# A wider tile cleared by GpSimd between two indirect transfers, in an attention-and-experts kernel

## The chip, the cores and the metric

One core of one Trainium2 chip runs the program. The metric is the device time of one launch in microseconds; lower is better. Two runs of the kernel before took 1105.46 and 1108.3 us, so its median is 1106.88 us. The profiled execution is a third run with its own time, 1112.21 us.

## The reference

Four batches of 10048 rows of 128 columns go through agent attention, and its rows then go through a two-level mixture of experts. Cut to what matters:

```python
a2k = sm(agents, k)                 # 49 agents attend to the keys
agent_v = a2k @ v
q2a = sm(q, agents)                 # each query attends to the 49 agents
x = (q2a @ agent_v).reshape(-1, 128)

g_idx = argmax(x @ w_group, axis=1)             # 4 groups, the best one per row
e_idx = argmax(xg @ w_expert[g], axis=1)        # 4 experts in it, the best one per row
h  = np.maximum(xg[mask_e] @ w1[g, e], 0.0)     # 128 -> 1024
ye = h @ w2[g, e]                               # 1024 -> 128
out[tok_idx] = combined[:, None] * ye           # by the row's two softmax weights
```

## The kernel before

**The natural part.** The rows of a batch lie in 79 tiles of 128. Each batch has one main expert, to which most of its rows go. For it the rows are taken in their natural order, four tiles (512 rows) at a time; this is what `natural` and `run` do. Such a unit has eight rounds. In a round `first` makes one 128 x 512 block of the hidden layer on TensorE (PE), two matmuls with a weight load each; ScalarE (ACT) writes its high half `hh` and VectorE (DVE) its low half `hl`, both in 16 bits. `second` multiplies the block of an earlier round with the second weights, twelve matmuls with a weight load each, into the accumulator `po`. So a round is 14 matmuls and 14 loads on PE. The finished unit is scaled by DVE into `oo` and leaves by an ordinary DMA from SyncE's queue.

**The rows that belong to other experts.** For the last batch handled (`LB`) the last part of the program, from about 770 us on, works by expert: 17 tiles (`TAKEN`) of up to 512 rows each. `fetch` (L1055) gathers a tile by four indirect DMAs from GpSimd (POOL), one for 128 rows of 200 bytes each, from a table `erow` in DRAM into `er` (five buffers). `turn` (L1082) transposes them on PE, `run` does the eight rounds, and `scatter` (L1092) scales the result into `oo` (three buffers, shared with the natural units) and sends it out by four indirect DMAs from POOL, 128 rows of 512 bytes each.

**The clearing between them.** After each of these indirect DMAs `apart` (L1074) puts one `memset` of a small tile `gap` on POOL. Nothing reads `gap`. `keep_in_program_order` keeps the DMA and the memset in the order in which they are written:

```python
def apart(ins):
    tc.keep_in_program_order(ins)
    tc.keep_in_program_order(pool.memset(gap, 0.0))
```

There are 68 gathers, 68 scatters and 136 memsets. POOL runs its instructions in order.

**The order of the work.** `build` ends with the loop that sets this order (L1236 to L1248): three tiles are fetched ahead, then two natural units of the batch before run, then for each of the 17 tiles its rounds run and the tile three places later is fetched; four more natural units are put between the 17. The rounds run with a lag (`LAG` is 8), so that a tile's `scatter` is issued while the next tile's rounds run. On POOL this gives 16 gathers with a memset behind each, four gathers with none between them (their memsets stand later in POOL's order), and from then on groups of four scatters and four gathers, each followed by its memset; at the end there are groups of four scatters alone.

Of the kernel before, what the change touches and what calls it, by code (L numbers as in the profile page):

```python
# [10 lines left out]
F32 = mybir.dt.float32  # L11
F16 = mybir.dt.float16
# [8 lines left out]
P = 128  # L21
# [111 lines left out]
def build(ctx, tc, qT, kT, v, agT, wr, w1, w2, cpk, out):  # L133
# [7 lines left out]
    const = ctx.enter_context(tc.tile_pool(name="const", bufs=1))  # L141
# [895 lines left out]

    done = [0]
    ring = []
    gap = const.tile([P, 16], F32, name="gap")  # L1040

    def place(b, col):
        for lo, hi, gidx, sidx in state[b]["idx"]:
# [235 lines left out]
```

## Time and profile before

| | |
|---|---|
| median of two runs | 1106.88 us |
| the profiled execution: device time | 1112.21 us |
| the profiled execution: span of its instructions | 1110.4 us |
| mean granted TensorE clock over the span | 0.936 |
| PE busy | 965.7 us (87%) |
| weight loads on PE's second row (PEld) | 753.1 us (68%) |
| DVE busy | 768.5 us (69%) |
| ACT busy | 639.3 us (58%) |
| POOL busy | 438.2 us (39%) |
| of which 136 memsets of `gap` | 17.9 us |
| first and last indirect DMA from POOL | 770.3 and 1102.7 us |

The device time is 1.8 us more than the span. Times in the views count from the span's start. In a row of the timeline the columns are the start, the duration, the engine, the line and operation, and in brackets how long the engine sat idle before it and what ended that; "issue" means that the profile shows nothing that it waited for. In a row of the windows each engine has its busy time in the stretch and in round brackets the number of its instructions; PE's matmuls and its weight loads (PEld) are counted apart, and after them come the granted clock, the share of DMA time, and GB/s.

### The profile page before, as it was taken

Reading aid. Unit: us, or ns where it says so; the run is one execution under the profiler, and the core shown is the slowest. Engines: PE = TensorE matmul, PEld = TensorE weight load, DVE = VectorE, ACT = ScalarE, POOL = GpSimd, SP = SyncE. Lnnn points to the kernel's source line nnn. Section 1 sums busy time; section 2 is a strip of 40 time slices with the busy share of each in tenths; the row PEclk is TensorE's granted clock in tenths of the full one; section 3 lists DMA queues with packets and bytes.
Section 4 is the critical chain, followed back from the end, with each engine's and each line's share of the span. In section 5 each row is a group of like instructions: output and inputs, shape, how many; then the busy total and the mean of one; then the engine's idle time right before and its main releaser. Section 6 shows DMA issues by size and latency. Waiting matters only on the chain.

```text
span 1110.4 us, 31414 instructions
## 1 busy us (share of the span) xinstructions
PE 965.7 (87%) x13174; PEld 753.1 (68%) x13174; DVE 768.5 (69%) x1475; ACT 639.3 (58%) x1144; POOL 438.2 (39%) x772
## 2 busy tenths in 40 slices
PE   4868989899999999989998999999597887877894
PEld 3747767678777887867787887776275665555673
DVE  6578889876989777797975679998263444434452
ACT  5355677798567787667766875544252333433441
POOL 3242283683054384026225520002506535454514
PEclk9969999999999999999998999999698788888988
DMA  9552254440475351157333112232243212232210
GB/s 297 164 184 84 73 150 142 137 146 21 141 237 151 103 153 37 33 183 264 110 99 99 53 31 79 94 125 81 63 181 104 99 62 100 65 102 65 91 55 31
DMA packets 104423, 124.58 MB, mean 112 GB/s; under 512 B 6743, under 2 KB 88152, under 8 KB 101328
## 3 DMA queue, kind: packets, MB, share of 16 engines
q1 hardware_dynamic: 99920, 116.57, 33.1%
q0 software_dynamic: 4352, 5.91, 2.0%
q8 instruction: 105, 1.72, 0.6%
q14 instruction: 46, 0.38, 0.1%
HBM read 89.01 MB, written 33.75 MB: 111 GB/s over the span
## 4 chain that ended last, share of the span: by engine, by line
PE 21%; issue 18%; POOL 13%; DVE 11%; ACT 1%; DMA 1%; POOLq 0%; SPq 0%; ACTq 0%
PE po L128 9%; PE ph L128 6%; POOL out L1097 6%; PE at L128 5%; DVE hl L128 5%; POOL er L1060 5%; POOL gap L1076 1%; POOL xl L237 1%; DVE oo L128 1%; DVE oh L128 1%; DMA w2f<-w 1%; DVE oa L128 0%; ACT hh L128 0%; DVE za L128 0%; DVE wbuf L128 0%
## 5 line engine op out<-in xcount | busy, mean ns | idle before, releaser
L128 DVE SCALAR_TENSOR_TENSOR hl<-ph,hh 128x512 f16<-128x512 f32 (+1 forms) x656 | 435.4, 678 | 246.0 <-ACT hh L128 182.6
L128 PEld LDWEIGHTS <-hh 128*128 128x128 f16 x5200 | 439.7, 100 | 197.7 <-issue 59.3
L128 ACT ACTIVATE hh<-ph 128x512 f16<-128x512 f32 (+1 forms) x656 | 381.1, 592 | 286.2 <-PE ph L128 249.3
L128 PE MATMUL po<-wbuf,hh 128*128 128x128 f16 x4816 | 495.5, 223 | 24.8 <-issue 24.3
L128 PE MATMUL po<-wbuf,hl 128*128 128x128 f16 x2408 | 451.9, 223 | 12.3 <-issue 12.2
L128 PE MATMUL ph<-et,wbuf 98*128 98x512 f16 (+1 forms) x1040 | 317.7, 385 | 25.7 <-DVE hl L128 20.3
L237 POOL TENSOR_TENSOR xl<-xf,xh 128x256 f16<-128x256 f32 (+1 forms) x288 | 191.2, 699 | 214.0 <-ACT xh L128 205.1
L128 PEld LDWEIGHTS <-hl 128*128 128x128 f16 x2600 | 260.5, 100 | 21.7 <-issue 19.3
L1097 POOL DMA_INDIRECT out<-oo,sidx x68 | 67.7, 996 | 164.9 <-DVE oo L128 155.6
L128 PEld LDWEIGHTS <-wbuf 98*128 98x128 f16 x1216 | 97.9, 100 | 46.9 <-issue 41.6
L1060 POOL DMA_INDIRECT er<-erow,gidx x68 | 69.3, 1019 | 127.4 <-DVE over L128 113.2
L128 ACT ACTIVATE xh<-xf 128x1024 f16<-128x1024 f32 x80 | 83.3, 1043 | 53.8 <-PE at L128 21.6
L379 POOL TENSOR_TENSOR sl<-S,sh 128x147 f16<-128x147 f32 (+1 forms) x90 | 45.4, 532 | 97.4 <-ACT sh L128 97.4
L128 PEld LDWEIGHTS <-xh 128*128 128x128 f16 x1264 | 61.3, 100 | 13.6 <-ACT xh L128 11.8
L582 POOL TENSOR_TENSOR rows<-ef,rows 128x147 f16<-128x147 f32 (+2 forms) x117 | 47.9, 439 | 46.9 <-ACT rows L128 46.7
L128 PE MATMUL ph<-ets,wbuf 98*128 98x512 f16 x176 | 58.1, 411 | 5.3 <-issue 3.1
L128 PEld LDWEIGHTS <-xl 128*128 128x128 f16 x632 | 53.5, 99 | 13.1 <-POOL xl L237 9.8
L128 PE MATMUL at<-agh,xl 128*128 128x49 f16 x538 | 54.3, 187 | 7.4 <-POOL xl L237 7.4
L128 PE MATMUL at<-agh,xh 128*128 128x49 f16 x538 | 54.6, 187 | 2.0 <-ACT xh L128 2.0
L128 PE MATMUL at<-agl,xh 128*128 128x49 f16 x538 | 54.4, 187 | 0.0
L128 PE MATMUL po<-wsg,hh 128*128 128x128 f16 x384 | 43.5, 235 | 5.4 <-issue 5.3
L128 DVE TENSOR_TENSOR oo<-po,cw 128x512 f32<-128x512 f32 (+1 forms) x65 | 43.8, 673 | 5.5 <-PE po L128 4.9
(288 smaller groups left out, 1054.8 us busy)
## 6 DMA issues: line engine op xcount, KB each, us to landing
xf<-kT SPq DMA_DIRECT2D x36, 512.0 KB
vf<-v SPq DMA_DIRECT2D x36, 512.0 KB
xf<-qT SPq DMA_DIRECT2D x36, 512.0 KB
out<-oo SPq DMA_DIRECT2D x62, 256.0 KB
wbuf<-wall SPq DMA_DIRECT2D x11, 1024.0 KB
wsg<-wall SPq DMA_DIRECT2D x6, 1024.0 KB
erow<-rows SPq DMA_DIRECT2D x3, 1975.0 KB
w1f<-w SPq DMA_DIRECT2D x7, 512.0 KB
```

The source lines that it names most:

```text
L128: return f(*a, **k)
L237: pool.tensor_sub(out=xl[:, y], in0=xf[:, y], in1=xh[:, y])
L379: pool.tensor_sub(out=sl[0:m, w], in0=x[:, j], in1=sh[0:m, w])
L582: (vec if early else pool).tensor_sub(out=rows[:, w, NA:2 * NA], in0=ef[:, y], in1=rows[:, w, 0:NA])
L1060: ins = pool.indirect_dma_start(out=er[:, q], out_offset=None, in_=erow[b][:, :], in_offset=bass.IndirectOffsetOnAxis(ap=place(b, j * w + ...
L1076: tc.keep_in_program_order(pool.memset(gap, 0.0))
L1097: ins = pool.indirect_dma_start(out=out, out_offset=bass.IndirectOffsetOnAxis(ap=place(x["b"], x["j"] * n + q)[1], axis=0), in_=o[:, q], i ...
```

## The change

The tile that `apart` clears gets 320 columns of 16 bits instead of 16 columns of 32 bits, so 640 bytes in each of 128 partitions instead of 64. It is a tile of its own in the pool of constants.

```diff
     done = [0]
     ring = []
-    gap = const.tile([P, 16], F32, name="gap")
+    gap = const.tile([P, 320], F16, name="gap")
```

Every engine has the same instructions in the same order as before; 136 memsets on POOL have another shape.

## The prediction

> **What bounds the kernel now.** I read the page's chain of work first, then the waits, the timeline of POOL and PE in the last stage, and windows that count instructions.
>
> ```profile
> span 1110.4 us, 31414 instructions
> PE 21%; issue 18%; POOL 13%; DVE 11%; ACT 1%; DMA 1%; POOLq 0%; SPq 0%; ACTq 0%
> ```
>
> The chain ends in POOL's indirect DMAs, and 18% of it is "issue", time with no visible cause. The waits show that POOL itself is mostly early:
>
> ```profile
> POOL out L1097 <- DVE oo L128: 155.6, 16, 37.8
> ```
>
> Sixteen of its 17 groups of scatters waited for results. So POOL does not set the pace; PE, which makes them, does. Its windows across one group of eight DMAs (834.19 to 844.4 us):
>
> ```profile
> 803.00:834.00 31.00, 31.00 (x393) 24.21 (x392) 22.40 (x34) 18.55 (x32) 0.00 (x0) 0.99 0.45 165
> ...
> 836.00:838.00 2.00, 2.00 (x29) 1.64 (x28) 1.29 (x2) 0.60 (x1) 1.73 (x4) 1.00 0.57 217
> 838.00:840.00 2.00, 1.54 (x22) 1.16 (x20) 0.00 (x0) 0.08 (x1) 1.73 (x3) 1.00 0.19 70
> 840.00:842.00 2.00, 0.95 (x8) 0.38 (x6) 0.04 (x1) 1.11 (x2) 1.70 (x4) 1.00 0.07 13
> 842.00:844.00 2.00, 0.49 (x3) 0.18 (x3) 0.65 (x1) 0.00 (x0) 1.76 (x3) 1.00 0.13 25
> 846.00:848.00 2.00, 2.00 (x15) 1.57 (x14) 1.73 (x3) 1.32 (x3) 0.00 (x0) 0.50 0.00 0
> ```
>
> With POOL idle (803 to 834) PE takes 393 matmuls and 392 loads in 31 us, 25.3 instructions per us, which is its full rate. Five microseconds into POOL's group it nearly stops, and it comes back when the group is over, at half clock (0.50). The DMA engines are nearly idle meanwhile (share 0.07 to 0.13), so this is not bandwidth. Other POOL work doesn't do it; from 384 to 404 us POOL computes for 17 of 20 us and PE runs at its rate:
>
> ```profile
> 384.00:404.00 20.00, 19.26 (x321) 15.59 (x319) 15.18 (x23) 16.84 (x31) 16.97 (x30) 1.00 0.48 132
> ```
>
> What PE lacks is instructions, as I read it. The counts fit a stock that drains:
>
> ```profile
> 834.22:839.18 4.96, 4.96 (x70) 4.00 (x67) 2.36 (x4) 1.74 (x3) 4.42 (x8) 1.00 0.63 233
> 923.70:930.91 7.21, 7.20 (x77) 5.53 (x75) 2.77 (x4) 2.12 (x4) 6.32 (x11) 0.82 0.48 183
> 839.45:845.50 6.05, 1.91 (x14) 0.95 (x14) 0.69 (x1) 1.19 (x2) 4.50 (x8) 0.91 0.11 28
> ...
> 834.19:1098.83 264.64, 215.51 (x2240) 158.39 (x2236) 112.80 (x172) 94.19 (x165) 127.43 (x228) 0.86 0.24 80
> ```
>
> From the start of POOL's group to the stop PE takes 137 instructions in 5.0 us, or 152 in 7.2 us where its clock was low: about the same count, not the same time. In the stop it gets 28 in 6.05 us, 4.6 per us. So a stock of about 137 - 23 = 115 runs out while 4.6 per us come in. The whole stretch from the first scatter to the last group has 4476 instructions, 176.9 us at full rate, and took 264.6: 87.7 us are lost. That is what bounds the stage.
>
> ```profile
> q8 instruction: 105, 1.72, 0.6%
> ```
>
> [...]
>
> **Do POOL's gaps feed PE?** The rows of the stop, POOL first:
>
> ```profile
> 839.06 0.13 POOL L1076 MEMSET gap<- 128x16 f32 x1
> 839.37 1.05 POOL L1060 DMA_INDIRECT er<-erow,gidx  x1 [0.18 <-issue]
> 840.43 0.12 POOL L1076 MEMSET gap<- 128x16 f32 x1
> 840.73 1.03 POOL L1060 DMA_INDIRECT er<-erow,gidx  x1 [0.17 <-issue]
> 841.75 0.12 POOL L1076 MEMSET gap<- 128x16 f32 x1
> ...
> 844.36 0.14 POOL L1076 MEMSET gap<- 128x16 f32 x1
> ...
> 1041.43 0.13 POOL L1076 MEMSET gap<- 128x16 f32 x1
> 1043.61 1.03 POOL L1060 DMA_INDIRECT er<-erow,gidx  x1 [2.04 <-issue]
> ```
>
> ```profile
> 839.86 0.22 PE L128 MATMUL po<-wsg,hl 128*128 128x128 f16 x1 [0.46 <-issue]
> 841.30 0.22 PE L128 MATMUL po<-wsg,hl 128*128 128x128 f16 x1 [0.68 <-issue]
> 842.74 0.22 PE L128 MATMUL po<-wsg,hl 128*128 128x128 f16 x1 [1.11 <-issue]
> 845.57 0.26 PE L128 MATMUL po<-wsg,hl 128*128 128x128 f16 x1 [1.08 <-issue]
> ```
>
> POOL's cycle is 1.0 us of DMA, 0.13 of memset, 0.18 until the next DMA: 1.31 us, a gap of 0.31. PE gets a small batch about 0.8 to 1.0 us after the start of each gap (839.06 to 839.86, 840.43 to 841.30, 841.75 to 842.74). So each gap seems to let 4.6 x 1.31 = 6 instructions through. What a longer gap lets through, one accident shows, the pause of 2.18 us at 1041.43:
>
> ```profile
> 1041.43:1043.61 2.18, 0.83 (x12) 0.58 (x10) 0.68 (x2) 1.36 (x4) 0.14 (x3) 1.00 0.06 16
> 1043.61:1048.56 4.95, 4.82 (x63) 3.91 (x62) 3.11 (x7) 1.84 (x4) 4.41 (x7) 1.00 0.51 171
> ```
>
> PE takes 22 instructions in it and 125 more before the next stop, of which 23 came in meanwhile: the pause brought 22 + 102 = 124. From 6 in 0.31 us to 124 in 2.18 us is 63 per us of added gap, if it is even; 6 in 0.31 us alone is 19 per us.
>
> **The change part by part.** Nothing is removed or moved. Each of 136 memsets grows.
>
> *The memset.* Not shown at this shape. The nearest rows:
>
> ```profile
> L1076 POOL MEMSET gap<- 128x16 f32 x136 | 17.9, 132 | 0.3
> L1272 POOL MEMSET const-float32-0.0<- 128x1 f32 x1 | 0.1, 99 | 0.2 <-issue 0.2
> L576 POOL CAST rows<-ef 128x392 f16<-128x392 f32 x1 | 0.7, 705 | 14.6 <-ACT ef L128 14.6
> ```
>
> From 1 to 16 columns 2.2 ns a column, from there to the cast's 392 columns 1.52. Above: 132 + 304 x 2.2 = 800 ns. If two 16-bit columns go as one: 132 + 144 x 1.52 = 350 ns. I take 450, between that and 132 + 304 x 1.52 = 595, because a fill reads nothing. Below: not under 132.
>
> *POOL's cycle.* The next DMA started 0.18 us after the memset's end, so I keep that: gap 0.63, cycle 1.63 us (1.53 to 1.98).
>
> *What a gap brings.* I take 45 per us of added gap, between 19 and 63 and nearer to the pause, whose interval contains the new gap: 6 + 0.32 x 45 = 20.5 per cycle.
>
> *A group of eight.* PE wants 25.3 x 1.31 = 33.1 per cycle, gets 6: 27.1 x 8 = 217 short, less the stock of 115, is 102, or 4.0 us; with 1.2 us from the last DMA's end to the restart (844.36 to 845.57), of which 0.1 brings instructions, 5.1. The trace: 6.05 us with 28 instructions, 4.9 lost. After: (41.2 - 20.5) x 8 = 166, less 115, is 51: 2.0 + 1.1 = 3.1 us. Saved 2.0 a group; some twelve such groups: -24 us.
>
> *The low clock.* Of the 87.7 us, twelve stops of 5 leave about 27 for the clock at half after each. In proportion to the stops (3.1 of 5.1): -11 us; their being too short to lower it at all would bring more, so I take -15.
>
> *The first 20 gathers.*
>
> ```profile
> 779.66:791.40 11.74, 4.31 (x19) 1.60 (x18) 1.35 (x2) 0.60 (x1) 10.16 (x18) 0.64 0.36 113
> 791.50:796.40 4.90, 0.92 (x4) 0.42 (x4) 0.00 (x0) 0.00 (x0) 3.96 (x4) 0.50 0.11 21
> ```
>
> With memsets PE gets 3.2 per us, in the four cycles without one 1.6, at nearly the same pitch. That speaks for the memset, not only the pause, letting instructions in. Before, 27.2 us want 688, and 20 x 6 + 115 come: 453 short, 17.9 us. After, 5.1 us longer: 817 wanted, 16 x 20.5 + 24 + 115 = 467 come, 13.8 us. -4 us.
>
> *The tail.*
>
> ```profile
> 1098.83 0.98 POOL L1097 DMA_INDIRECT out<-oo,sidx  x1 [1.92 <-DVE oo L128]
> ```
>
> Nothing hides the last four scatters: three longer gaps, +1 us.
>
> *POOL's own length.* A tile costs it 8 x 1.63 = 13.0 us, and a tile comes every 264.6/16 = 16.5 us, after the change every 14.1: it still fits, with little to spare. The gathers have cover:
>
> ```profile
> L1060 POOL DMA_INDIRECT er<-erow,gidx x68: 993/1003/1213, 770.3 to 1046.3; - x68
> L128 PE MATMUL at<-ident,er x68: 219/219/219, 809.7 to 1075.8; 128*98 128x128 f16 x68
> ```
>
> The last was issued at 1046.3 and PE transposes its tile at 1075.8.
>
> Sum: -24 - 15 - 4 + 1 = -42 us on the profiled 1112.2, so 1070. The median is 5.3 lower: **1065 us**.
>
> *Ends.* At 63 per us: 26.2 a cycle, a loss of 1.3 us per group, -46 - 20 - 8 + 1 = -73; but POOL at 13.0 plus about 0.2 a tile allows only 264.6 - 211 = 53 of the first two, so -60: 1047. With the 350 ns memset POOL needs 12.2 a tile and allows 66: 1030 if all goes well. At 19 per us: 12 a cycle, 5.8 us lost per group, +8 + 1 + 1: 1117. With 800 ns and 19: 18.7 a cycle, 6.5 lost, +17 + 3 + 2: 1129.
>
> **The rivals.**
>
> *Gaps count, not their length.* If each gap passes one batch of 6 however long it is, PE is short (41.2 - 6) x 8 - 115 = 167, 6.6 + 1.1 = 7.7 us a group: +31, first gathers +5, tail +1: **1144 us**. The place is the gap after each DMA; it decides where an added microsecond brings fewer than 25.3 instructions, PE's own rate. For it: the batches come one per cycle. Against: the pause, and the rows without memset.
>
> *The fill is long and POOL becomes the bound.* At 800 ns the cycle is 1.98 us and a tile needs 15.8 us of POOL. PE is fed (at 45 per us, 36 of 50 a cycle), but tiles come every 16.0: -8, first gathers -8, tail +2: **1093 us**. For it: the slope between the two memsets. Against: the cast's.
>
> *Nothing moves.* Two of the gathers without a memset:
>
> ```profile
> 791.47 1.00 POOL L1060 DMA_INDIRECT er<-erow,gidx  x1 [0.18 <-issue]
> 792.77 1.00 POOL L1060 DMA_INDIRECT er<-erow,gidx  x1 [0.30 <-issue]
> ```
>
> Near break-even, or the fill hides in the 0.3 us that lies between two DMAs without a memset too: **1107 us**. Against: before, the next DMA always came after the memset.
>
> **How the numbers follow.** My forecast 0.60, the counted gaps 0.14, POOL as bound 0.10, nothing 0.16. A measurement can tell about 2% from no change, 22 us, so faster means under 1085. The forecast is that in nearly all of its spread (0.58), POOL as bound half the time (0.05; 1093 lies just outside): faster 0.63. Same: the rest of these (0.02 + 0.05), nothing (0.15): 0.22. Slower: 0.14 and a little: 0.15. Range 1030 to 1125: below the shortest memset with the richest gap, above a value between the two ends at 19 per us (1117, 1129); it leaves out the rival at 1144. The forecast's own is 1030 to 1090.
>
> **What would show it.** Right: the memset at 0.35 to 0.6 us, POOL's cycle at 1.5 to 1.8, batches of 15 or more per cycle, stops of about 3 us instead of 6, less time at clock 0.50 between 834 us and the end, and tiles every 14 us. Wrong: stops as long as POOL's group minus 5 us, with batches still of 6; or a memset of 0.8 us with POOL busy from tile to tile.

## The result and the profile after

The changed kernel takes 1022.94 us (median of two runs, 1022.78 to 1023.11). Against 1106.88 us that is a ratio of 0.9242, with a 95% interval of 0.919 to 0.9293: faster by 84 us, where 42 were forecast. The profiled execution took 1022.78 us, 89.4 less than the one shown of before; its page:

```profile
span 1020.9 us, 31414 instructions
...
PE 33%; DVE 14%; POOL 7%; issue 4%; ACT 2%; DMA 2%; POOLq 0%; SPq 0%; ACTq 0%; DVEq 0%
...
L1076 POOL MEMSET gap<- 128x320 f16 x136 | 52.3, 384 | 0.3
```

"issue", time without a visible cause, fell from 18% of the chain to 4%, and PE's share of it rose from 21% to 33%. A memset takes 384 ns where 132 were taken before. POOL's timeline inside a group, and the scatters at which the first group, the second and the last one begin (start, duration, operation, idle time ahead of it):

```profile
820.45 1.01 POOL L1097 DMA_INDIRECT out<-oo,sidx  x1 [17.57 <-DVE oo L128]
...
826.60 1.05 POOL L1060 DMA_INDIRECT er<-erow,gidx  x1 [0.16 <-PE ph L128]
827.66 0.38 POOL L1076 MEMSET gap<- 128x320 f16 x1
828.20 1.03 POOL L1060 DMA_INDIRECT er<-erow,gidx  x1 [0.17 <-issue]
...
832.88 1.03 POOL L1097 DMA_INDIRECT out<-oo,sidx  x1 [0.17 <-issue]
...
1008.73 0.98 POOL L1097 DMA_INDIRECT out<-oo,sidx  x1 [0.17 <-issue]
```

The next DMA starts 0.17 us after the memset's end (0.18 before), so the gap between two DMAs is 0.55 us and POOL's cycle is 1.55 us (eight of them from 820.45 to 832.88). Windows of the changed kernel, read as those of before: busy time and number of matmuls, then of weight loads, and the granted clock as the third value from the end.

```profile
774.70:793.50 18.80, 18.42 (x224) 13.83 (x222) 15.09 (x22) 12.23 (x21) 16.75 (x25) 1.00 0.52 179
772.98:797.86 24.88, 23.98 (x287) 17.90 (x286) 17.74 (x28) 14.25 (x25) 22.33 (x32) 1.00 0.62 223
...
820.45:825.45 5.00, 5.00 (x71) 4.04 (x68) 3.08 (x5) 3.23 (x6) 4.50 (x7) 1.00 0.64 236
825.45:832.85 7.40, 7.40 (x96) 5.72 (x94) 4.55 (x7) 3.29 (x7) 6.58 (x10) 1.00 0.47 163
...
820.45:870.00 49.55, 46.87 (x578) 35.76 (x575) 29.16 (x44) 24.77 (x43) 44.37 (x64) 1.00 0.36 119
...
820.45:1006.97 186.52, 179.19 (x2240) 138.74 (x2236) 112.84 (x171) 94.75 (x165) 155.28 (x226) 1.00 0.35 112
1006.97:1020.90 13.93, 0.00 (x0) 0.00 (x0) 0.69 (x1) 0.00 (x0) 6.87 (x11) 0.63 0.10 31
```

The rows from 820.45 to 832.85 are the place where the kernel before stopped. The group begins at 820.45; 139 instructions go in the first 5 us, and then, where 28 came in 6.05 us before, 190 come in 7.4 us: 25.7 per us, the full rate. The whole stage has the same 4476 instructions as before and takes 186.5 us instead of 264.6, at clock 1.00 throughout; 9.6 us are lost against full rate instead of 87.7. In the first gathers (first row) PE gets 446 instructions in 18.8 us, 23.7 per us; before it got 3.2 per us once its stock had run out. Up to 115 of the 446 can have come from the stock. The second row is all 16 gathers with a long gap: 573 instructions.

What a gap of 0.55 us brings can only be bounded here, since PE was not short. The row from 820.45 to 870.00 holds 32 indirect DMAs without a break: 1153 instructions, of which at most 115 are stock, so the gaps brought at least 1038 / 32 = 32 per cycle. The waits say that POOL, early 16 times before, now is early six times:

```profile
POOL out L1097 <- DVE oo L128: 29.2, 6, 17.6
```

From the first scatter to the last group's first one it issues 64 scatters and 48 gathers; 112 cycles of 1.55 us are 173.6 us, against 176.9 us that PE needs at full rate. The two are level now.

The 89.5 us of span come from these stretches (before, after): from the first gather (at 770.31, at 772.98) to the first scatter 63.9 and 47.5 us, -16.4; from there to the last group (1098.83, 1008.73) 264.6 and 188.3 us, -76.4; the last group and what follows 11.6 and 12.2, +0.6; and the first gather came 2.7 us later.

### The profile page after: what moved, and what is told of

It is laid out like the page before. It is cut to its first block, busy times and chain, and to the rows that moved or that the text cites. A ratio compares the mean times of both kernels' runs of the same rounds, so it can differ in the third digit from the quotient of the medians.

```text
span 1020.9 us, 31414 instructions
## 1 busy us (share of the span) xinstructions
PE 925.2 (91%) x13174; PEld 731.0 (72%) x13174; DVE 768.9 (75%) x1475; ACT 639.6 (63%) x1144; POOL 472.4 (46%) x772
## 4 chain that ended last, share of the span: by engine, by line
PE 33%; DVE 14%; POOL 7%; issue 4%; ACT 2%; DMA 2%; POOLq 0%; SPq 0%; ACTq 0%; DVEq 0%
PE po L128 16%; PE ph L128 12%; DVE hl L128 6%; PE at L128 5%; POOL out L1097 3%; POOL gap L1076 2%; DMA xf<-kT 2%; POOL er L1060 1%; POOL xl L237 1%; ACT hh L128 1%; DVE oo L128 1%; DVE oh L128 1%; DVE oa L128 1%; DVE za L128 0%; ACT vh L128 0%
## 5 line engine op out<-in xcount | busy, mean ns | idle before, releaser
L128 PEld LDWEIGHTS <-hh 128*128 128x128 f16 x5200 | 426.4, 98 | 153.7 <-issue 8.3
L128 PE MATMUL po<-wbuf,hh 128*128 128x128 f16 x4816 | 476.7, 220 | 0.8 <-issue 0.5
L128 PE MATMUL po<-wbuf,hl 128*128 128x128 f16 x2408 | 438.7, 220 | 0.9 <-issue 0.7
L128 PE MATMUL ph<-et,wbuf 98*128 98x512 f16 (+1 forms) x1040 | 312.8, 380 | 25.0 <-DVE hl L128 22.2
L128 PEld LDWEIGHTS <-hl 128*128 128x128 f16 x2600 | 254.2, 98 | 3.8 <-issue 1.4
L1060 POOL DMA_INDIRECT er<-erow,gidx x68 | 69.3, 1018 | 126.7 <-DVE over L128 113.6
L128 PEld LDWEIGHTS <-xh 128*128 128x128 f16 x1264 | 60.9, 100 | 14.0 <-ACT xh L128 12.2
L128 PE MATMUL ph<-ets,wbuf 98*128 98x512 f16 x176 | 52.8, 379 | 3.0 <-issue 1.3
L1076 POOL MEMSET gap<- 128x320 f16 x136 | 52.3, 384 | 0.3
```

Of the source, the lines that this page charges most:

```text
L128: return f(*a, **k)
L1060: ins = pool.indirect_dma_start(out=er[:, q], out_offset=None, in_=erow[b][:, :], in_offset=bass.IndirectOffsetOnAxis(ap=place(b, j * w + ...
```

## The experiments

**The theory** is the prediction's: PE takes its instructions from a stock that is hardly refilled while POOL issues indirect DMAs, and what refills it is the time between two of them. **Its rivals**: it is the memset, or its address or shape, and not the time; the stock is a time and not a count of instructions; the time may lie anywhere on POOL. The runs went to six chips, here by their numbers; the chip of the first comparison is not on record. The time of the kernel before differs from chip to chip: 1109.49 us on chip 11, 1111.71 on chip 9 and 1117.74 on chip 8, but 1002.41 on chip 10, 1001.26 on chip 14 and 1003.09 on chip 15. So every ratio is against runs of the kernel before on the same chip, and the chips on which it takes 1001 to 1003 us are a finding of their own.

### Chip 11, where PE stops

**No memset at all.**

```diff
         tc.keep_in_program_order(ins)
-        tc.keep_in_program_order(pool.memset(gap, 0.0))
```

> The kernel before without any memset between indirect DMAs. Theory (a stretch in which POOL generates no descriptors lets PE's instructions in, and the memset is part of that stretch): the four gathers of before that had no memset gave PE 2.1 instructions per cycle instead of 6, so a group of eight is (33.1 - 2.1) x 8 - 115 = 133 short, 5.3 + 1.2 us instead of 5: about 1125 us. Rival (only the time from one DMA's end to the next start counts, and that is 0.30 us with and without a small memset): 1107 us.

Measured: 1100.57 us, ratio 0.9916 (0.989 to 0.9941). POOL's timeline, then windows from a group's start to the stop, of the stop, and over the first gathers and the last four of them:

```profile
840.09 1.02 POOL L1060 DMA_INDIRECT er<-erow,gidx  x1 [0.31 <-issue]
841.41 1.00 POOL L1060 DMA_INDIRECT er<-erow,gidx  x1 [0.30 <-issue]
```

```profile
833.54:838.64 5.10, 5.10 (x73) 4.14 (x69) 2.39 (x4) 1.77 (x3) 3.98 (x4) 1.00 0.61 238
838.64:846.30 7.66, 4.54 (x32) 2.49 (x30) 1.44 (x3) 2.46 (x5) 4.06 (x4) 0.78 0.10 22
...
779.66:791.40 11.74, 5.16 (x21) 1.68 (x21) 1.40 (x3) 1.20 (x2) 9.00 (x10) 0.58 0.37 113
791.50:796.40 4.90, 1.21 (x7) 0.61 (x6) 0.00 (x0) 0.00 (x0) 3.82 (x4) 0.50 0.13 21
```

Without the memset the gap is still 0.30 us, and the stop comes after 142 instructions, where it was 137. In the first gathers PE gets 42 in the stretch in which it got 37 with the memsets. So a memset of 16 columns does not help PE; its 0.13 us hides in a pause of 0.30 us that POOL makes without it too. What the theory says of descriptors is an assumption: no trace shows what POOL does in the 1.0 us of an indirect DMA. The rival's 1107 us was nearer than the theory's 1125, by which the memset itself lets instructions in. The gain of 0.8% was not traced to a place; in the one stop shown PE got rather more while the DMAs ran (30 in 3.86 us from 838.64 to 842.50, against 27 in 4.91 us from 839.45 to 844.36 before).

**Three memsets instead of one.**

```diff
-        tc.keep_in_program_order(pool.memset(gap, 0.0))
+        for _ in range(3):
+            tc.keep_in_program_order(pool.memset(gap, 0.0))
```

> The kernel before with three memsets of 16 columns after each DMA instead of one. The last memsets of before follow each other every 0.17 us, so the gap is 0.13 + 2 x 0.17 + 0.18 = 0.65 us and the cycle 1.65. Theory (the length of the gap counts): PE is fed as in the changed kernel, POOL's 120 DMAs from the first scatter on take 198 us instead of 186: 1030 to 1040 us. Rival (the size of what is cleared, or the length of one instruction, counts): the stops stay and POOL's groups are longer, 1107 to 1145 us.

Measured: 1105.52 us, 0.9965 (0.9943 to 0.9988). The timeline shows that it did not make the gap that it was written for:

```profile
839.64 1.00 POOL L1060 DMA_INDIRECT er<-erow,gidx  x1 [0.18 <-issue]
840.64 0.12 POOL L1077 MEMSET gap<- 128x16 f32 x1
840.95 1.00 POOL L1060 DMA_INDIRECT er<-erow,gidx  x1 [0.18 <-issue]
841.95 2.83 POOL L1077 MEMSET gap<- 128x16 f32 x17
```

```profile
831.76:836.80 5.04, 5.04 (x71) 4.08 (x68) 2.39 (x4) 1.77 (x3) 4.48 (x8) 1.00 0.58 231
836.80:843.19 6.39, 3.16 (x20) 1.32 (x18) 0.69 (x1) 1.20 (x2) 5.30 (x15) 0.86 0.11 26
```

One memset stays between two DMAs, and the other 17 of a group's 24 run behind it in one piece. The stops are those of before, 38 instructions in 6.39 us. The edit missed its aim, and still answers one rival: 2.8 us of memsets behind the group's last DMA bring nothing. What a gap made of something other than one long memset would do stays untested.

**A fill in between: 160 columns of 32 bits.**

```diff
-    gap = const.tile([P, 16], F32, name="gap")
+    gap = const.tile([P, 160], F32, name="gap")
```

> 160 columns of 32 bits: the same bytes as in the changed kernel, half the columns. If the fill goes by columns, 132 + 144 x 0.83 = 250 ns, cycle 1.43 us; if by bytes, 384 ns and the time of the changed kernel, 1023 us. At 250 ns, theory with an even rate per us of added gap (138 or more, from the changed kernel): at least 22 of the 36 instructions a cycle, so a group of eight loses no more than its stock; 1010 to 1045 us. Rival (a threshold between a gap of 0.43 and 0.55 us): stops as before, 1100 to 1120 us.

Measured: 1069.31 us, 0.9644 (0.9611 to 0.9677). The memsets (shortest, median and longest in ns), and the windows of a group up to its stop, of the stop, and of the whole stage from the first scatter to the last group:

```profile
L1076 POOL MEMSET gap<- x136: 231/250/270, 770.7 to 1054.8; 128x160 f32 x136
```

```profile
826.68:832.66 5.98, 5.98 (x83) 4.78 (x80) 2.70 (x5) 2.97 (x5) 5.32 (x9) 1.00 0.55 208
832.66:838.30 5.64, 3.66 (x34) 1.83 (x31) 1.76 (x3) 1.19 (x2) 4.70 (x8) 1.00 0.07 14
...
826.68:1049.65 222.97, 192.82 (x2240) 140.00 (x2236) 112.17 (x172) 93.65 (x165) 141.29 (x228) 0.99 0.30 95
```

The same 640 bytes a partition as in the change take 250 ns and not 384: the fill went by columns and not by bytes, 118 ns over the 16-column one for 144 more columns of 32 bits, 0.82 ns each, and 252 ns for 304 more of 16 bits, 0.83 ns each. With a gap of 0.42 us and a cycle of 1.42 the stop comes a microsecond later, and in it PE gets 65 instructions in 5.64 us, 11.5 per us or 16 per cycle. In the first trace it was 6: 10 more for 0.11 us more of gap. The stage takes 223.0 us, between the 264.6 and the 188.3 of the first comparison. The time lies in neither range that was expected: an even rate, bounded from below by the changed kernel, gave at most 1045 us, a threshold at least 1100.

**Fewer instructions for the same time.** Two matmuls of 128 columns become one of 256, so a round has 10 matmuls and loads in place of 14. The kernel leaves out a sum by this: the low product is written beside the high one instead of being added to it, so its output is not the reference's.

```diff
-                pe.matmul(o, hh[:, s], wt[:, 0:C], start=(k == 0 and j == 0 and q == 0), stop=False)
-                pe.matmul(o, hh[:, s], wt[:, C:2 * C], start=False, stop=False)
+                o2 = po[:, q // 2 * 2:q // 2 * 2 + 2].rearrange("p a c -> p (a c)")
+                pe.matmul(o2, hh[:, s], wt, start=(k == 0 and j == 0 and q == 0), stop=False)
```

> The kernel before with the first two products of a round's twelve (high half with high and with low weights) made as one matmul of 256 columns, so a round has 10 matmuls and loads instead of 14 for the same columns. It writes the low product beside the high one instead of adding it, so the sums are not the reference's. Theory (PE runs out of a stock of about 115 instructions): 18.1 instructions per us at full rate, so the stock lasts 115 / (18.1 - 4.6) = 8.5 us from the start of POOL's group instead of 5.0, and a group's loss is 2.6 us instead of 5. Rival (something holds PE's execution from a fixed time into the group): the stop starts at 5.0 us and ends with the group, as before.

Measured: 1070.8 us in one run. Windows of two groups up to their stop, and of the first stop:

```profile
819.38:826.57 7.19, 7.19 (x71) 5.42 (x69) 3.08 (x5) 3.03 (x6) 6.29 (x11) 1.00 0.44 172
826.57:832.15 5.58, 1.64 (x14) 0.91 (x11) 1.44 (x3) 1.92 (x4) 2.77 (x6) 1.00 0.21 29
...
884.17:891.37 7.20, 7.20 (x72) 5.43 (x71) 3.08 (x5) 2.97 (x6) 6.31 (x11) 1.00 0.49 182
```

The stop begins after 140 and 143 instructions, as it did after 137 before, but at 7.2 us instead of 5.0. So what runs out is a number of instructions and not a time. The stop was expected at 8.5 us, from 18.1 instructions per us; PE took 19.5 per us in this stretch, with which the same stock of 115 would last 7.7.

### Chips 10, 14 and 15, where the kernel before takes 1001 to 1003 us

Four variants went to chip 10: a fill of 240 columns, one of 384, the long fill behind the gathers alone (32 columns behind a scatter), and 320 columns on 16 partitions.

```diff
+    gap = const.tile([P, 240], F16, name="gap")
...
+    gap = const.tile([P, 384], F16, name="gap")
...
+        tc.keep_in_program_order(pool.memset(gap[:, 0:n], 0.0))
...
+        tc.keep_in_program_order(pool.memset(gap[0:16], 0.0))
```

> The changed kernel with 240 columns of 16 bits. The fills measured so far (16 columns 0.13 us, 160 columns of 32 bits 0.25, 320 of 16 bits 0.38) lie on a line of 0.83 ns a column, so the fill takes 0.32 us, the gap is 0.49 and the cycle 1.49. Theory A (what a gap lets in rises evenly between 14 instructions at 0.42 us and 39 or more at 0.55): about 27 of the 38 that PE wants per cycle, short by less than the stock in one group of eight, but POOL's groups nearly join: 1025 to 1050 us. Theory B (a threshold just under 0.55 us): stops as with 160 columns, 1060 to 1072 us.

> The changed kernel with 384 columns: fill 0.44 us, gap 0.61, cycle 1.61 us. Theory (PE is fed at 0.55 us already, and POOL's 120 DMAs from the first scatter on, 186 us at 1.55, are as long as PE's work): 120 x 1.61 = 193 us, so 1028 to 1034 us. Rival (PE still lacks instructions at 0.55 us, longer is better): below 1020 us.

> The changed kernel with 320 columns behind the gathers only, 32 behind the scatters. POOL's DMAs from the first scatter on take 52 x 1.55 + 68 x 1.32 = 170 us, less than PE's 177. Four scatters leave PE 4 x 27 = 108 short, just inside its stock of 115. Theory A (a gap of 0.55 us brings more than the 39 that PE takes in a cycle, so the stock is refilled during the gathers): no stops, 1008 to 1020 us. Theory B (it brings just about 39): the stock stays empty once it has run out, and each group of scatters costs about 4 us: 1050 to 1075 us.

> The changed kernel, but the memset clears 320 columns of the first 16 partitions only, an eighth of the bytes. Theory (only the time between two DMAs counts): the fill takes as long per partition, 0.38 us, and the kernel 1018 to 1028 us. Rival (what counts is that all of POOL's lanes write, or how much is written): stops come back, 1060 to 1107 us.

Measured, in this order: 1004.83 us, 1.0029 (1.0008 to 1.0049); 1013.43 us, 1.0115 (1.008 to 1.015); 1003.31 us, 1.002 (0.9994 to 1.0046); 1004.68 us, 1.0027 (1.0002 to 1.0052). There was nothing to tell apart, since the kernel before took 1002.41 us there; in the trace with 240 columns PE takes 3547 instructions from 817.33 to 955.47 us, 25.7 per us. So on chip 14 both kernels were run again, with a tile of 320 columns of which 32 are cleared, and the 16 partitions:

```diff
+    gap = const.tile([P, 320], F16, name="gap")
...
+        tc.keep_in_program_order(pool.memset(gap[:, 0:32], 0.0))
```

> The kernel before, unchanged, for its profile on this chip. On one chip it took 1109 us, on another 1002. Theory C (PE's supply of instructions during POOL's indirect DMAs differs from chip to chip): if this chip gives about 1105, PE stops 5 us into each of POOL's groups, with 4 to 5 instructions per us; if it gives about 1002, PE runs through POOL's groups at 24 to 25 instructions per us with the same gaps of 0.31 us. Rival (the stops are there on every chip, and the chips differ elsewhere): stops at about 1002 us too.

> The changed kernel, unchanged, beside the one before on the same chip. Theory C: about 1020 us where the one before takes about 1105; where that takes about 1002, there is nothing to gain and POOL's longer cycle costs some us: 1005 to 1012 us. Rival (the gain came from two different chips in the first comparison): the two kernels within 1.5% of each other on every chip, at 1105 or at 1005 us.

> The changed kernel's tile of 320 columns, but only 32 of them (64 bytes, as before) are cleared: the addresses of the change with the time of before. Theory (the time of the fill counts): the time of the kernel before on this chip, within 1%. Rival (what counts is where the tiles behind the larger one lie in SBUF): the time of the changed kernel.

> The changed kernel, the memset on the first 16 partitions alone (fill 0.354 us on another chip). Where the kernel before has stops: theory (only the time between two DMAs counts): 1018 to 1035 us; rival (all lanes must write): 1060 to 1107 us. Where the kernel before has none: 1003 to 1008 us, which tells nothing.

Measured: 1001.19 us, 0.9999 (0.9983 to 1.0015); 1008.63 us, 1.0064 (1.0038 to 1.0089); 1004.25 us, 1.0036 (1.0016 to 1.0057); 1004.59 us, 1.0036 (1.0019 to 1.0052). The kernel before on chip 14, its timeline, its window over four groups of eight DMAs without a break, its waits, and its last scatter:

```profile
818.04 0.13 POOL L1076 MEMSET gap<- 128x16 f32 x1
818.34 0.99 POOL L1097 DMA_INDIRECT out<-oo,sidx  x1 [0.18 <-issue]
```

```profile
817.02:858.78 41.76, 41.76 (x537) 32.87 (x534) 27.69 (x42) 24.03 (x41) 36.22 (x64) 1.00 0.41 141
```

```profile
POOL out L1097 <- DVE oo L128: 43.0, 6, 18.0
```

```profile
995.02 0.98 POOL L1097 DMA_INDIRECT out<-oo,sidx  x1 [0.18 <-issue]
```

The DMAs have the same gaps of 0.3 us and PE takes 1071 instructions in 41.76 us, 25.6 per us, its full rate, where on chips 11 and 9, with gaps of 0.30 to 0.31 us, it stops after 5.0 to 5.1 us. The changed kernel there, in the last three of these views:

```profile
817.10:961.33 144.23, 144.23 (x1855) 114.08 (x1853) 96.48 (x146) 82.19 (x142) 128.84 (x185) 1.00 0.42 132
```

```profile
POOL out L1097 <- DVE oo L128: 15.0, 1, 15.0
```

```profile
999.24 0.98 POOL L1097 DMA_INDIRECT out<-oo,sidx  x1 [0.17 <-issue]
```

PE is at full rate here too (3708 in 144.23 us, 25.7 per us), but POOL has only the first wait for results left: it runs almost without a break, falls behind and ends later. PE's last matmul starts at 989.6 us before and 989.5 after, and POOL's last scatter 4.2 us later. The fill is a plain cost, 0.6% at 320 columns and 1.2% at 384 on chip 10. On chip 15 the change and the large tile with a short fill were put together once more:

> The changed kernel once more, beside the kernel before on the same chip. Where the kernel before takes about 1105 us (a chip with stops): theory (the longer fill lets instructions in) 1018 to 1030 us, ratio about 0.925; rival (the first comparison mixed two chips) about 1105 us. Where it takes about 1001 us: 1005 to 1012 us.

> The changed kernel's tile with 32 of its 320 columns cleared. On a chip with stops: theory (the length of the fill) 1095 to 1110 us, as before; rival (the addresses behind the larger tile) 1018 to 1030 us, as the changed kernel. On a chip without stops: 1000 to 1006 us.

Measured: 1009.3 us, 1.0049 (1.0028 to 1.007), and 1004.15 us, 1.0011 (0.9991 to 1.0032). No view of this chip shows PE's instructions; the mean clock over the span is 0.971 and 0.976 in these two, 0.977 for the kernel before on chip 14, and 0.936 for it in the first comparison, where PE stops.

### Chip 9: the change, and its tile with a short fill

The edit of the second is that of the 32 cleared columns above.

> The changed kernel beside the kernel before. On a chip with stops (before about 1105 us): theory (the longer fill) 1018 to 1030 us; rival (the first comparison mixed two chips) about 1105 us. On a chip without: 1005 to 1012 us against 1001.

> The changed kernel's tile with 32 of 320 columns cleared. On a chip with stops: theory (the length of the fill) 1095 to 1110 us; rival (the addresses behind the larger tile) 1018 to 1030 us. On a chip without: 1000 to 1006 us.

Measured: the change 1021.13 us, 0.9186 (0.916 to 0.9213); the large tile with 32 cleared columns 1113.51 us, 1.0032 (1.0007 to 1.0057). Windows of the latter's first group and stop:

```profile
834.66:839.64 4.98, 4.98 (x69) 4.02 (x67) 2.39 (x4) 1.77 (x3) 4.48 (x8) 1.00 0.62 242
839.64:846.09 6.45, 2.18 (x20) 1.22 (x17) 0.69 (x1) 1.19 (x2) 4.69 (x9) 0.85 0.12 26
```

136 instructions, then 37 in 6.45 us: the picture of before. So neither the tile nor where it lies makes the gain; the length of the fill does. And since both kernels were timed on this one chip, the 8% of the first comparison is not a difference between chips.

### Chip 8: half of the gaps, and fewer partitions

The long fill behind gathers only, 32 columns behind scatters; and 320 columns on 16 partitions:

```diff
-    def apart(ins):
+    def apart(ins, n=320):
         tc.keep_in_program_order(ins)
-        tc.keep_in_program_order(pool.memset(gap, 0.0))
+        tc.keep_in_program_order(pool.memset(gap[:, 0:n], 0.0))
...
-                apart(ins)
+                apart(ins, 32)
```

> 320 columns behind the gathers only, 32 behind the scatters. On a chip with stops: theory A (a gap of 0.55 us brings more than the 39 instructions that PE takes in a cycle, so the stock is refilled during the gathers) 1008 to 1030 us; theory B (just about 39, the stock stays empty) 1050 to 1085 us. On a chip without: 1000 to 1006 us, as on the first such chip.

> The memset clears 320 columns of the first 16 partitions only; fill 0.354 us. On a chip with stops: theory (only the time between two DMAs counts) 1018 to 1035 us; rival (all lanes of POOL must be at work, or the bytes count) 1060 to 1112 us. On a chip without: 1003 to 1008 us.

Measured for the first: 1090.51 us, 0.975 (0.9689 to 0.9811): some gain, and unclear whether it is 2%. Both expected ranges (1008 to 1030 and 1050 to 1085 us) were missed. Its windows over the first gathers up to the stop and in it, then over a group up to its stop, and two halves of another stop:

```profile
770.52:786.45 15.93, 15.89 (x185) 11.54 (x184) 10.87 (x19) 9.24 (x16) 14.26 (x21) 1.00 0.49 165
786.45:795.50 9.05, 6.75 (x78) 4.77 (x76) 5.79 (x8) 3.38 (x7) 8.14 (x12) 1.00 0.75 238
...
824.06:829.10 5.04, 5.04 (x71) 4.07 (x67) 2.40 (x4) 1.78 (x3) 4.53 (x8) 1.00 0.60 236
...
843.62:846.62 3.00, 1.11 (x11) 0.67 (x10) 0.00 (x0) 0.00 (x0) 2.66 (x5) 1.00 0.12 30
846.62:849.62 3.00, 1.92 (x15) 1.00 (x14) 0.69 (x1) 1.20 (x2) 2.67 (x5) 0.79 0.13 17
```

In a group the stock runs out during the four scatters, after 138 instructions in 5.04 us, as the short gaps of 0.31 us there give little. The four gathers behind them have gaps of 0.55 us, yet PE gets 7 per us in the first three microseconds and 9.7 in the next. In the first gathers, which in this kernel are those of the changed one up to 795.5, a gap of the same length gives more: 154 in 9.05 us with the stock empty, 17 per us or 26 per cycle. So the same gap brought 11 to 15 instructions per cycle in one place and 26 in another. That a longer gap helps late and not at once, and that a half group is too short for it, is a reading of these few rows and not shown. From the same 16 gathers the changed kernel got 573 instructions without a stop in the first comparison, and this kernel 523 here (369 + 154, 770.52 to 795.50) with one: less a stock of 115, at least 28.6 per cycle there and 26 here. So this chip gave a little less, in one trace of each.

Measured for the second: 1061.27 us, 0.9489 (0.9434 to 0.9544). Its memset and its windows:

```profile
L1076 POOL MEMSET gap<- 16x320 f16 x136 | 48.3, 355 | 0.3
```

```profile
820.84:826.86 6.02, 6.02 (x81) 4.70 (x77) 2.39 (x4) 2.65 (x5) 5.38 (x8) 1.00 0.50 193
826.86:834.15 7.29, 5.06 (x52) 3.08 (x49) 2.82 (x5) 2.78 (x6) 5.50 (x8) 1.00 0.20 32
...
854.65:871.91 17.26, 13.40 (x136) 8.53 (x134) 7.59 (x11) 6.39 (x11) 15.43 (x24) 1.00 0.28 87
```

On an eighth of the partitions the fill takes 355 ns, 29 less, so the gap is 0.52 us. In its stops PE gets 13.9 and 15.6 per us, 21 to 24 per cycle of 1.53, close to the 26 that a gap of 0.55 gave on this chip. The time misses the theory's range (1018 to 1035 us) and lies at the edge of the rival's (1060 to 1112), by which the number of partitions written or the bytes count. The theory's range came from other chips, though, and the changed kernel itself was not run on chip 8. The length of the gap can account for the time within what these few stops tell; that the number of partitions adds something is not shown and not excluded.

No variant beats both kernels on both kinds of chip. Where PE stops, the changed kernel has the lowest ratio (0.9242 and 0.9186; it was not run on chips 8 and 11); where it does not, nothing measured faster than the kernel before. The changed kernel itself still takes 1021 to 1023 us where the kernel before stops, and 1009 where it does not.

## Why the prediction was wrong, step by step

**What bounds the kernel: right.** On chips 8, 9 and 11, as in the first comparison, PE stops after about 140 instructions of a group of indirect DMAs (136 to 143 in the rows shown at clock 1.00 and gaps of 0.30 to 0.31 us), by count and not by time (137 in 5.0 us, 140 and 143 in 7.2 us in the kernel with wider matmuls). That it is instructions which it lacks is still a reading: PE is idle with no visible cause, and the count is what stays constant. The time between the DMAs feeds it: an empty 0.30 us is worth as much as one with a short memset (a stop after 142 instructions and after 137), the 32-column fill of the large tile changes nothing (ratio 1.0032, a stop after 136), the 320-column fill removes the stops (4476 instructions in 186.5 us). Longer gaps were only made with one longer memset, so the time and the length of that instruction are not told apart.

**"What a gap brings": this step failed.** The prediction took 45 instructions per us of added gap, between 19 and 63 and "nearer to the pause", with 63 as the upper end. Measured: in the first comparison, where PE was not short, at least 32 per cycle with 0.55 us, (32 - 6) / 0.24 = 108 per us; with 0.42 us on chip 11 16 per cycle, (16 - 6) / 0.11 = 91. On chip 8 it was (21 - 6) / 0.21 = 71 with 0.52 us and (26 - 6) / 0.24 = 83 with 0.55, but in the half group shown only about 13 per cycle (50 in 6.0 us), or 29 per us, so no single rate holds everywhere. (The 6 is that of the first trace throughout.) The pause of 2.18 us could not show this, and the trace's own numbers said why: after it PE took 125 instructions until the next stop, nearly as many as after a long idle stretch (137 at 834). The pause had all but filled the stock, so most of its 124 were the stock's size and no rate. A floor was used as a ceiling.

**The groups and the low clock: -39 forecast, -76.4 measured.** With at least 32 of the 39.2 that PE wants in a cycle of 1.55 us, a group is at most (39.2 - 32) x 8 = 58 short, less than the stock of 115, and the windows show no stop. The prediction's own sum then gives all of the twelve stops and all 27 us of low clock, about 87, of which 76.4 came; the remainder is in the 9.6 us that the stage still loses and in the 1.8 us from PE's last matmul to the last group's first scatter. The clock is 1.00 through the whole stage. Nor does its loss go "in proportion to the stops": with 160 columns the stops are still 5.6 us long, and the clock over the stage is 0.99 where it was 0.86, with 11.5 instructions per us in the stop shown instead of 4.6.

**The first gathers: -4 forecast, -16.4 measured**, for the same reason. The argument there, that 3.2 per us with memsets and 1.6 without show the memset letting instructions in, fell with the kernel without memsets: 42 instructions in that stretch with none at all, against 37. With no memset anywhere the last four cycles still got less, 13 in 4.9 us; so their place and not the missing memset is the likelier reason.

**The memset: 450 ns taken, 384 measured**, and 0.17 us to the next DMA as taken; the cycle became 1.55 us instead of 1.63. The bounds of 350 and 800 held it.

**The cap by POOL was too low.** It let the stage shrink by 53 us at most, from 16 tiles of eight DMAs each at 1.63 us. Five tiles are gathered ahead of the stage, so four of its 16 tiles have scatters alone: there are 112 DMAs between the two ends and not 128, and at 1.55 us they need 173.6 us and not 211. That cap is what held the lower end of the range at 1030.

**The tail: +1 forecast, +0.6 measured.** The first gather's start, 2.7 us later, was in no term; the memset behind it starts at 773.4 us with both kernels on chip 14, at 771.8 there with the large tile and 32 columns, and at 771.3 to 775.6 in the four traces of chip 10, so it is spread between executions.

**The rivals.** That gaps count and not their length is refuted by the fills that made gaps of 0.42 and 0.55 us. POOL as the bound holds on chip 14, where the traces show no stop: the change costs 0.6% there, and 0.5% on chip 15; the fill that it supposed, 800 ns, was not there. "Nothing moves" is what happens with a tile whose fill stays short.

**What no step had:** that on some chips there are no stops. Nothing in the trace of one chip could have told it. The trace of before from chip 14 has the same gaps of 0.3 us on POOL and no stop, with 25.6 instructions per us through four of its groups.

**Open.** Why chips differ, and what PE waits for in a stop. Each chip was visited once, so the chip is not told apart from whatever else differed between the visits. The DMA queue that the page calls "instruction" does not show it: the page of the kernel before on chip 14 has the same packets and bytes there as the one of the first comparison:

```profile
q8 instruction: 105, 1.72, 0.7%
```

0.7% of 16 engines' 1002.8 us, or 0.6% of 1110.4 us before, is about 1 us a packet on both; as a mean over the run it could hide single late packets. The change was not run on chip 8 as it stands.

## What to carry to other kernels

Where an engine has work and the profile names nothing that it waits for, count its instructions in windows. Here the count until a stop was nearly constant (137, and 140 and 143 with wider matmuls) at varying times (5.0 and 7.2 us); it was read as a stock that runs out, and the gain lay with POOL, which was busy in every stop shown. When one accidental long pause is to give a rate, ask first whether it has filled something: then it gives a size, and the rate is only bounded from below. And a kernel that is tuned around such a stop may be tuned to some chips only: run the kernel before on several before a fill of this kind is kept, since it paid 8% in the first comparison and on chip 9 and cost 0.6 and 0.5% on chips 14 and 15.

## What was not expected of the hardware

- The same kernel takes 1106 to 1118 us on some chips and 1001 to 1003 us on others, with equal instructions; on the first PE stops after 136 to 142 instructions in the traces with gaps of 0.30 to 0.31 us between POOL's indirect DMAs, on chip 14 it takes 25.6 per us with the same gaps and no trace shows a stop.
- GpSimd's fill went by columns: 132 ns for 16 and 250 for 160 of 32 bits, 317, 384 and 438 ns for 240, 320 and 384 of 16 bits, 0.82 to 0.85 ns a column. On 16 partitions 320 columns take 355 ns.
- Without any memset POOL left 0.30 us between two indirect DMAs, about as much as the 0.31 us with a memset of 16 columns.
